# A dynamic convolution in eight 64x32 array tiles instead of four 128x32 ones, from block 8 on

## The chip, the cores and the metric

The kernel runs on one core of one Trainium2 chip. A core has five engines that run side by side and meet through semaphores: TensorE (PE, matrix products; a weight load, PEld, and a matmul are separate instructions), VectorE (DVE), ScalarE (ACT), GpSimd (POOL) and SyncE (SP), of which the last mostly issues DMAs. SBUF is the on-chip memory of 128 partitions. TensorE writes into PSUM[...]. The metric is the device time of one execution in microseconds (us). Before the change it is 747.56 us, the median of three runs (747.36 to 747.77).

## The reference

The input x has 8 sequences of 4096 tokens with 192 channels in 8 heads of 24. Each token has, per head, seven weights of its own; they go through a softmax and weigh the token and the six before it. What results goes through a feed-forward network with a squared ReLU.

```python
w = exp(weight_gen - max);  w = w / (sum(w) + 1e-9)        # (B, S, 8 heads, 7 taps)
out = einsum('bshk,bskhg->bshg', w, windows_of_7(x))       # causal, zeros ahead of the start
h = maximum(out.reshape(-1, 192) @ w_in, 0)                # (32768, 2048)
return h * h @ w_out                                       # (32768, 192)
```

## The kernel before

**Ranges and blocks.** The 32768 tokens are cut into 64 ranges of 512 tokens (`TB`). Blocks 0 and 1 (`BLOCKS`) have one range each, blocks 2 to 32 two. The first range of a two-range block goes to partitions 0 to 63 of the convolution's result y and the second to partitions 64 to 127 (`half`), for three groups of 64 channels (`NK`).

**Convolution as matmuls.** A range is covered by five tiles of 128 tokens (`NT`), which start 104 tokens apart (`STEP`), 24 tokens ahead of the range; each gives 104 output tokens (96 the last). For one tile the convolution is a product of x (tokens on partitions, channels as the stationary columns) with a band matrix bd: column c holds, for one head, the seven weights of output token c at the rows of the tokens that it takes. `st_band` (L338) makes bd on VectorE, by multiplying the weights wr, broadcast, with the constant `mask`, which has ones in a band seven rows wide. Two neighbouring heads lie interleaved in bd's columns, so a matmul reads every second element. Heads of 24 channels don't match strips of 32: for each strip `conv_pieces` (L370) gives first a matmul over 32 channels with the later head's band, and then one over the first 8, 16 or 24 channels with the earlier head's band, which overwrites those rows. Each is a matmul that starts and stops by itself.

**Array tiles before.** A conv matmul (L416) uses all 128 rows of the array and 32 of its columns, at `tile_position=(0, p0)`, where `p0 = RT * half + 32 * (q % 2)` takes four values: four column tiles, used in turn. A two-range block has 5 tiles x 3 channel groups x 2 heads x 4 = 120 matmuls, into two PSUM tiles yp of two banks each. ScalarE then copies them to y in fp16 (L432), the first 128x1024, the second 128x512.

**Feed-forward.** A unit u (`st_unit`, L437) makes 128 of the 2048 hidden channels for the block's 1024 tokens: six matmuls h (L446) of 64 rows and 512 columns, pairs of row halves side by side in different PSUM banks, then the ReLU to t on ScalarE (L455) and the square to g on VectorE (L458). There are 16 units in a two-range block. A step M is half of a quarter of the block's second product: 32 matmuls o (L480) of 64 rows and 192 columns; at the end of a quarter ScalarE (L494) and VectorE (L496) add the two row halves to o_sb, and SP stores them. PSUM has three h tiles of two banks, which h and yp share (`ps_h`), and two banks for o.

**Order.** It is written out by hand: `steady` gives "MuMuuu" three times and then "MuuuMCu" for a block, where C is the convolution of the next block, so it stands between the block's 15th and 16th unit. C is followed by the x loads of the block after (`x_load`, on the POOL queue, with a cast to fp16, into two tiles xt). The bands of the next block (B) stand at units 5 and 9 or 1 and 5, later for a few early blocks. The weights come from a softmax in pieces (E on ScalarE, S on VectorE), which is stored to DRAM (vd) from where SP reads wr in the banded layout (`block_load`, L286): one row of 64 values per token, five tiles in one DMA; where a range starts a sequence, or ends a part of the softmax, the first or last tile has a DMA of its own. For the first blocks the weights go from SBUF to SBUF instead (`wr_load_sbuf`).

**Start-up.** POOL makes `mask` and others with memsets and selects and then clears `v_big`, before the first DMAs that it issues.

Of the kernel before, what the change touches and what calls it, by code (L numbers as in the profile page):

```python
# [9 lines left out]
def kernel(  # L10
# [26 lines left out]
    nc = tc.nc  # L37
    f32 = mybir.dt.float32
    f16 = mybir.dt.float16

    B, S, D = x.shape
    H, KK = weight_gen.shape[2], weight_gen.shape[3]
# [3 lines left out]
    HP = H // 2  # L46

    P = 128
    TB = 512
    NBB = S // TB  # L50
    NSUB = B * NBB
    BLOCKS = [(0, 1), (1, 1)] + [(n, 2) for n in range(2, NSUB, 2)]
# [5 lines left out]
    SL = 8  # L58
    RT = 64
    NK = D // RT  # L60

    NT = 5
    STEP = 104
    BASE = -24
    starts = [BASE + STEP * i for i in range(NT)]
    bounds = [0, 104, 208, 312, 416, TB]

    AluOp = mybir.AluOpType
    AxisX = mybir.AxisListType.X
    ActF = mybir.ActivationFunctionType  # L70

    const = ctx.enter_context(tc.tile_pool(name="const", bufs=1))
# [5 lines left out]
    p_bd = ctx.enter_context(tc.tile_pool(name="p_bd", bufs=3))  # L78
    p_y = ctx.enter_context(tc.tile_pool(name="p_y", bufs=2))
# [4 lines left out]
    ps_h = ctx.enter_context(tc.tile_pool(name="ps_h", bufs=3, space=bass.MemoryType.PSUM))  # L84
# [5 lines left out]
    w_i = const.tile([P, WQ, 2, NQ + NQ // 2], f16, name="w_i")  # L90
    w_o = const.tile([P, NF, Dm], f16, name="w_o")
    mask = const.tile([P, P, 2], f16, name="mask")
    swap = const.tile([P, P], f16, name="swap")
    FIRST = 8
    PARTS = {0: (8, 8, 8, 8), 1: (8, 8, 16), 2: (16, 16)}
# [14 lines left out]
    def band_mask():  # L110

        nc.gpsimd.memset(mask, 1.0)
        for sign, base in ((1, 0), (-1, KK - 1)):
            nc.gpsimd.affine_select(
                out=mask, in_=mask, pattern=[[sign, P], [0, 2]], compare_op=AluOp.is_ge,
                fill=0.0, base=base, channel_multiplier=-sign,
            )


# [148 lines left out]
    x_t, wr_t, bd_t, yp_t, y_t, g_t, h_t, t1_t, o_t, o_sb_t = ({} for _ in range(10))  # L268

    def rows(ap2d, t0, width):  # L270

        return bass.AP(
            tensor=ap2d.tensor, offset=ap2d.offset + t0 * width,
            ap=[[width, P], [STEP * width, NT], [1, width]],
        )

    def ends(b):
        rs = PARTS.get(b, (R,))
        return [P * sum(rs[: i + 1]) for i in range(len(rs))]

    def tile_start(j, i):

        t1 = (j % NBB + 1) * TB
        return TB - P if i == NT - 1 and t1 in ends(j // NBB) else starts[i]

    def block_load(j, dst, src, width, eng):  # L286
        t0 = (j % NBB) * TB
        first, last = int(t0 == 0), NT
        if first:
            eng.dma_start(out=dst[:, 0], in_=src[0:P, :])  # L290
        a = t0 + tile_start(j, NT - 1)
        if a != t0 + starts[-1]:
            last = NT - 1
            eng.dma_start(out=dst[:, last], in_=src[a : a + P, :])
        ap = rows(src, t0 + starts[first], width)
        ap = bass.AP(
            tensor=ap.tensor, offset=ap.offset,
            ap=[ap.ap[0], [STEP * width, last - first], ap.ap[2]],
        )
        eng.dma_start(out=dst[:, first:last], in_=ap)  # L300
# [63 lines left out]
    quads = []  # L364
    for q in range(D // 32):
        ha, hb = (32 * q) // G, (32 * q + 31) // G
# [3 lines left out]
    def conv_pieces(j):  # L370


        s0, n = BLOCKS[j]
        th = n * TB // 2
        halves = []
        for half in (0, 1):
            s, a = (s0 + half, 0) if n == 2 else (s0, th * half)
            halves.append([
                (s, i, half, max(bounds[i], a), min(bounds[i + 1], a + th), a)
                for i in range(NT) if bounds[i] < a + th and bounds[i + 1] > a  # L380
            ])
        if n == 2:
            for k in range(NK):
                for later in (True, False):
                    for pair in zip(*halves):
                        for s, i, half, a, b, base in pair:
                            for q in (2 * k, 2 * k + 1):
                                yield later, s, i, q, half, a, b, base
        else:
            for pair in zip(*halves):  # L390
                for later in (True, False):
                    for k in range(NK):
                        for s, i, half, a, b, base in pair:
                            for q in (2 * k, 2 * k + 1):
                                yield later, s, i, q, half, a, b, base

    def st_conv(j):

        n = BLOCKS[j][1]
        th = n * TB // 2  # L400
        per = 1024 // th
        y = p_y.tile([P, NK, TB], f16, name="y")
        y_t[j] = y
        yps = [
            ps_h.tile([P, 2 * TB], f32, name="yp", tag="h") for _ in range(-(-NK // per))
        ]
        for later, s, i, q, half, a, b, base in conv_pieces(j):
            lo = bounds[i]
            hi = lo + (STEP if tile_start(s, i) == starts[i] else bounds[i + 1] - lo)
            _, ha, hb, pre = quads[q]  # L410
            m, h = (32, hb) if later else (pre, ha)
            bd = bd_t[s][:, H * lo : H * hi].rearrange("p (g c e) -> p g e c", g=HP, e=2)
            p0 = RT * half + 32 * (q % 2)
            k = q // 2
            col = th * (k % per) - base
            nc.tensor.matmul(  # L416
                out=yps[k // per][p0 : p0 + m, col + a : col + b],
                lhsT=x_t[s][:, i, 32 * q : 32 * q + m],
                rhs=bd[:, h // 2, h % 2, a - lo : b - lo],
                start=True,  # L420
                stop=True,
                skip_group_check=True,
                tile_position=(0, p0),
            )
        for n, yp in enumerate(yps):
            k0, k1 = n * per, min((n + 1) * per, NK)

            copies = ((k0, k1, nc.scalar.copy),)
            if j == 0:
                copies = ((0, 2, nc.scalar.copy), (2, NK, nc.vector.tensor_copy))  # L430
            for a, b, copy in copies:
                copy(  # L432
                    out=y[:, a:b, 0:th],
                    in_=yp[:, (a - k0) * th : (b - k0) * th].rearrange("p (k c) -> p k c", c=th),
                )
# [70 lines left out]
        )  # L506

    def st_bands(j):
        first = int(j % NBB == 0)
        last = NT - int(tile_start(j, NT - 1) != starts[-1])  # L510
        for tiles in (range(first), range(first, last), range(last, NT)):
            if tiles:
                st_band(j, tiles)

    with nc.allow_low_precision("fp16 matmul pipeline"), tc.manual_schedule():
# [3 lines left out]
        for b in range(B):  # L519
            t0 = 0  # L520
# [25 lines left out]
        s0, s1, s2 = parts[:3]  # L546
# [76 lines left out]
        for n, s in enumerate(parts[4:], 4):  # L623
            b, f = s.b, s.fb
            k = n - min(m for m, p in enumerate(parts) if p.b == b)
# [8 lines left out]
        for j in range(len(plans), NBLK - 1):  # L634
            a = BLOCKS[j + 1][0]
# [61 lines left out]
        for j in range(NBLK):  # L697
# [3 lines left out]
            for step in plans[j].split():  # L701
                kind, n = step[0], int(step[1:] or 0)
# [24 lines left out]
        j = NBLK - 1  # L727
# [44 lines left out]
```

The softmax here doesn't subtract the row's maximum and nothing guards it: scores larger than these inputs give would overflow.

## Time and profile before

| | |
|---|---|
| median of three runs | 747.56 us |
| span of the profiled execution | 746.6 us |
| TensorE clock granted | full, all through |
| busy: PE, PEld, DVE, ACT, POOL | 738.7, 556.1, 621.7, 624.4, 89.3 us |
| h matmuls (L446) | 3168, 380.3 us busy |
| o matmuls (L480) | 8032, 385.4 us busy |
| conv matmuls (L416) | 3864, 52.0 us busy |
| ReLU (L455) / square (L458) | 512 each, 1026 / 687 ns |
| bands (L348) | 89, 149.3 us busy |
| copies of y on ScalarE (L432) | 64, 47.9 us busy |
| instructions read by DMA for PE (queue q8) | 118 packets, 1.93 MB |

The profile is one execution. Busy time of PE is the time in which at least one matmul is in the array by the modelled ends of matmuls; matmuls overlap, so starts tell more than lengths. The chain that ended last is followed back from the last instruction, at each step to what released it or to the instruction before it on its engine. A group row reads: line, engine, operation, output<-input, shape, count | busy us, mean ns of one | idle time of the engine ahead of it, and who ended most of it. The median of runs also holds what lies around the span, 0.9 us.

### The profile page before, as it was taken

The page shows a single profiled execution, that of the slowest core. Times are in us where ns is not written, and L with a number is a line of the kernel's source. Part 1 is how long each engine was busy: PE and PEld are TensorE (multiplying, and loading weights), DVE is VectorE, ACT ScalarE, POOL GpSimd, SP SyncE. Part 2 cuts the span into 40 slices and gives each one's busy share as a digit, 9 for nine tenths or more (in the row PEclk, how much of TensorE's full clock was granted, in tenths as well). Part 3 has the DMA queues.
Part 4 walks back from the last instruction along what each step waited for, and adds up shares of the span by engine and source line. Part 5 has one row for each costly group of instructions (what it writes and reads, how often), then busy time and mean ns, then how long its engine had stood idle before and what let it go on. Part 6 is the DMA issues. An engine that isn't in the chain of part 4 may idle for free.

```text
span 746.6 us, 33289 instructions
## 1 busy us (share of the span) xinstructions
PE 738.7 (99%) x15106; PEld 556.1 (74%) x15106; DVE 621.7 (83%) x1002; ACT 624.4 (84%) x755; POOL 89.3 (12%) x130
## 2 busy tenths in 40 slices
PE   8999999999999999999999999999999999999998
PEld 4767777777777778777877777777778777777787
DVE  5999998998889888887889888898888987677853
ACT  4998888898888888888888888888888888888884
POOL 7322220101101100011000110001100011000000
PEclk9999999999999999999999999999999999999999
DMA  7745444436554234643245442265341354432312
GB/s 214 121 97 119 80 86 99 99 72 139 94 118 80 73 59 80 139 79 73 40 80 139 94 72 56 48 139 108 59 80 46 59 108 80 60 70 52 53 46 65
DMA packets 122169, 64.81 MB, mean 87 GB/s; under 512 B 83849, under 2 KB 118636, under 8 KB 121516
## 3 DMA queue, kind: packets, MB, share of 16 engines
q1 hardware_dynamic: 77708, 45.66, 22.3%
q0 software_dynamic: 44176, 16.93, 20.5%
q8 instruction: 118, 1.93, 1.1%
q14 instruction: 23, 0.19, 0.1%
q10 hardware_dynamic: 144, 0.10, 0.0%
HBM read 48.61 MB, written 28.70 MB: 104 GB/s over the span
## 4 chain that ended last, share of the span: by engine, by line
PE 91%; DVE 4%; DMA 2%; ACT 2%; issue 1%; DVEq 0%; ACTq 0%; SPq 0%
PE o L480 43%; PE h L446 42%; PE yp L416 6%; DVE bd L348 2%; DVE g L458 1%; ACT t L455 1%; DMA vd<-v_big 1%; DMA wr<-v_first 1%; DMA wg<-in_weight_gen_dram 0%; DVE v_big L239 0%; ACT ex L217 0%; DVE o_sb L496 0%; DVE ssum L224 0%; DVE rcp L231 0%; DVE v_first L239 0%
## 5 line engine op out<-in xcount | busy, mean ns | idle before, releaser
L455 ACT ACTIVATE t<-h 128x1024 f16<-128x1024 f32 x512 | 496.7, 1026 | 64.5 <-PE h L446 63.9
L458 DVE TENSOR_TENSOR g<-t 128x1024 f16<-128x1024 f16 x512 | 334.1, 687 | 99.1 <-ACT t L455 96.4
L480 PEld LDWEIGHTS <-g 64*128 64x128 f16 (+1 forms) x8032 | 352.5, 94 | 54.2 <-issue 3.8
L480 PE MATMUL o<-w_o,g 64*128 64x192 f16 (+1 forms) x8032 | 385.4, 243 | 0.2
L446 PE MATMUL h<-y,w_i 64*128 64x512 f16 (+1 forms) x3168 | 380.3, 370 | 1.9 <-ACT t L455 0.8
L446 PEld LDWEIGHTS <-w_i 64*128 64x128 f16 x3168 | 162.5, 94 | 117.5 <-issue 5.2
L348 DVE TENSOR_TENSOR bd<-wr,mask 128x4160 f16<-128x4160 f16 (+3 forms) x89 | 149.3, 1701 | 4.2 <-DMA wr<-v_first 4.2
L300 POOL DMA_DIRECT2D xt<-in_x_dram x62 | 51.6, 836 | 445.6 <-PE yp L416 422.7
L494 ACT COPY o_sb<-o 128x384 f32<-128x384 f32 x129 | 62.2, 482 | 33.7 <-PE o L480 33.7
L496 DVE TENSOR_TENSOR o_sb<-o,o_sb 128x384 f32<-128x384 f32 x123 | 68.2, 554 | 8.2 <-ACT o_sb L494 5.6
L432 ACT CAST y<-yp 128x1024 f16<-128x1024 f32 (+1 forms) x64 | 47.9, 799 | 15.1 <-PE yp L416 15.0
L416 PE MATMUL yp<-bd,xt 128*32 128x104 f16 (+8 forms) x3864 | 52.0, 208 | 0.7 <-DVE bd L348 0.3
L416 PEld LDWEIGHTS <-xt 128*32 128x32 f16 (+3 forms) x3864 | 46.2, 92 | 7.1 <-issue 6.4
L239 DVE TENSOR_TENSOR v_big<-ex,rcp 128x112 f16<-128x112 f32 (+1 forms) x136 | 27.3, 264 | 2.1 <-DMA vd<-v_big 0.9
L217 ACT ACTIVATE ex<-wg 128x448 f32<-128x448 f32 (+2 forms) x44 | 27.2, 618 | 2.1 <-DMA wg<-in_weight_gen_dram 2.1
L224 DVE TENSOR_REDUCE ssum<-ex 128x64 f32<-128x448 f32 (+2 forms) x44 | 26.1, 593 | 2.6 <-ACT ex L217 2.6
L231 DVE RECIPROCAL rcp<-ssum 128x64 f32<-128x64 f32 (+2 forms) x44 | 23.7, 539 | 1.5
L290 POOL DMA_DIRECT2D xt<-in_x_dram x7 | 3.8, 548 | 137.1 <-PE yp L416 137.1
L330 POOL DMA_DIRECT2D wr<-v_first x31 | 16.8, 559 | 16.1 <-DVE v_first L239 15.9
L544 PE MATMUL wp<-warm 128*128 128x512 f16 x39 | 10.7, 440 | 1.3 <-DVE warm L536 1.3
L544 PEld LDWEIGHTS <-warm 128*128 128x128 f16 x39 | 4.2, 111 | 7.1 <-issue 2.6
L239 DVE TENSOR_TENSOR v_first<-ex,rcp 128x112 f16<-128x112 f32 (+1 forms) x48 | 9.1, 255 | 0.3
(25 smaller groups left out, 28.7 us busy)
## 6 DMA issues: line engine op xcount, KB each, us to landing
out_dram<-o_sb SPq DMA_DIRECT2D x63, 384.0 KB, 3.0
xt<-in_x_dram POOLq DMA_DIRECT2D x42, 240.0 KB, 6.2
wg<-in_weight_gen_dram SPq DMA_DIRECT2D x4, 1064.0 KB, 8.3
xt<-in_x_dram POOLq DMA_DIRECT2D x20, 192.0 KB, 5.4
wr<-vd SPq DMA_DIRECT2D x38, 80.0 KB, 3.9
vd<-v_big SPq DMA_DIRECT2D x5, 512.0 KB, 5.5
wg<-in_weight_gen_dram SPq DMA_DIRECT2D x5, 392.0 KB
wg<-in_weight_gen_dram SPq DMA_DIRECT2D x3, 616.0 KB, 4.5
```

The source lines that it names most:

```text
L217: nc.scalar.activation(out=self.ex[:, lo:hi].rearrange("p r g k e -> p (r g) k e"), in_=self.wg[:, lo:hi].rearrange("p r (g e) k -> p (r g ...
L239: eng.tensor_tensor(out=bass.AP(tensor=v.tensor, offset=v.offset + lo * H * SL + lo % SL * 2 + g * SL * 2, ap=[list(v.ap[0]), [H * SL + 2, ...
L300: eng.dma_start(out=dst[:, first:last], in_=ap)
L348: nc.vector.tensor_tensor(out=bd_t[j][:, H * lo : H * (lo + len(tiles) * n)].rearrange("p (g m c) -> p g m c", g=shape[1], c=2 * SL), in0= ...
L416: nc.tensor.matmul(out=yps[k // per][p0 : p0 + m, col + a : col + b], lhsT=x_t[s][:, i, 32 * q : 32 * q + m], rhs=bd[:, h // 2, h % 2, a - ...
L432: copy(out=y[:, a:b, 0:th], in_=yp[:, (a - k0) * th : (b - k0) * th].rearrange("p (k c) -> p k c", c=th),)
L446: nc.tensor.matmul(out=h[:, half, jj * th : (jj + 1) * th], lhsT=w_in_chunk(u * per + jj, slot, half), rhs=y_t[j][r0 : r0 + RT, k, 0:th], ...
L455: nc.scalar.activation(out=t1, in_=h, func=ActF.Relu)
L458: nc.vector.tensor_tensor(out=g, in0=t1, in1=t1, op=AluOp.mult)
L480: nc.tensor.matmul(out=oo[:, cc * Dm : (cc + 1) * Dm], lhsT=g[r0 : r0 + n, cc * P : (cc + 1) * P], rhs=w_o[r0 : r0 + n, fc, :], start=(fc ...
L494: nc.scalar.copy(out=o_sb, in_=o[0][:, c])
L496: nc.vector.tensor_tensor(out=o_sb, in0=o[1][:, c], in1=o_sb, op=AluOp.add)
```

## The change

From block 8 on (ranges 14 to 63, 25 blocks) the convolution is laid out otherwise; blocks 0 to 7 stay.

- A range is cut into two segments of 256 tokens (`SEG`). Partitions 0 to 63 of xt and wr hold tiles of the first segment, 64 to 127 of the second. A tile has 64 tokens (`RT`) and gives 56 outputs (`SSTEP`; 32 the last), after 8 tokens of lead-in; there are again five.
- `split_load` replaces `block_load` for these: one DMA for each segment, with first or last tiles apart where a sequence starts or a part ends; in the first case a memset on POOL clears the eight rows ahead of the sequence.
- `st_split_band` makes a band of 5 x 56 columns for all 8 heads at once, 2240 values per partition for 4160, with `smask`, the diagonal blocks of `mask`, which POOL copies at start-up.
- `st_split_conv` has 240 matmuls of 64 rows for 120 of 128 rows, at `tile_position=(r0, p0)` with r0 0 or 64: eight tiles, used in turn. The row halves write to different PSUM banks (`yp[..., r, ...]`). The first copy of y is issued ahead of the last third of the matmuls; the copies have the same sizes as before.

```diff
+    SPLIT = 8
+    SEG = TB // 2
+    SSTEP = 56
+    LEAD = 8
+    sbounds = [SSTEP * i for i in range(NT)] + [SEG]
...
+        for r0 in (0, RT):
+            nc.gpsimd.tensor_copy(
+                out=smask[r0 : r0 + RT], in_=mask[r0 : r0 + RT, r0 : r0 + RT]
+            )
...
+    def last_shift(j):
+
+        return (RT - sbounds[-1] + sbounds[-2]) if (j % NBB + 1) * TB in ends(j // NBB) else LEAD
+
+    def split_load(j, dst, src, width, eng):
+
+        for r in (0, 1):
+            t0 = (j % NBB) * TB + SEG * r
+            d = dst[RT * r : RT * (r + 1)]
+            first, last = int(t0 == 0), NT
+            if first:
+                nc.gpsimd.memset(d[0:LEAD, 0], 0.0)
+                eng.dma_start(out=d[LEAD:, 0], in_=src[0 : RT - LEAD, :])
+            if last_shift(j) != LEAD:
+                last = NT - 1
+                eng.dma_start(out=d[:, last], in_=src[t0 + SEG - RT : t0 + SEG, :])
+            eng.dma_start(
+                out=d[:, first:last],
+                in_=bass.AP(
+                    tensor=src.tensor,
+                    offset=src.offset + (t0 + SSTEP * first - LEAD) * width,
+                    ap=[[width, RT], [SSTEP * width, last - first], [1, width]],
+                ),
+            )
+
     def block_load(j, dst, src, width, eng):
+        if is_split(j):
+            return split_load(j, dst, src, width, eng)
...
+    def st_split_band(j):
+
+        bd_t[j] = p_bd.tile([P, H * NT * STEP], f16, name="bd")
+        n = H * SSTEP
+        for i0, i1, shift in (
+            ((0, NT, LEAD),) if last_shift(j) == LEAD
+            else ((0, NT - 1, LEAD), (NT - 1, NT, last_shift(j)))
+        ):
+            cols = SSTEP if i1 - i0 > 1 else sbounds[-1] - sbounds[-2]
+            shape = (P, HP * (i1 - i0), cols // SL, 2 * SL)
+            nc.vector.tensor_tensor(
...
+                op=AluOp.mult,
+            )
+
+    def st_split_conv(j):
+
+        s0 = BLOCKS[j][0]
+        y = p_y.tile([P, NK, TB], f16, name="y")
+        y_t[j] = y
+        for k0, k1 in ((0, 2), (2, NK)):
+            yp = ps_h.tile([P, 2, TB], f32, name="yp", tag="h")
+            for k in range(k0, k1):
+                for later in (True, False):
+                    for i in range(NT):
+                        a, b = sbounds[i], sbounds[i + 1]
+                        for half in (0, 1):
+                            for q in (2 * k, 2 * k + 1):
+                                _, ha, hb, pre = quads[q]
+                                m, h = (32, hb) if later else (pre, ha)
+                                for r in (0, 1):
+                                    r0 = RT * r
+                                    p0 = RT * half + 32 * (q % 2)
+                                    col = SEG * (k - k0)
+                                    bd = bd_t[s0 + half][
+                                        r0 : r0 + RT, H * SSTEP * i : H * SSTEP * (i + 1)
+                                    ].rearrange("p (g c e) -> p g e c", g=HP, e=2)
+                                    nc.tensor.matmul(
+                                        out=yp[p0 : p0 + m, r, col + a : col + b],
+                                        lhsT=x_t[s0 + half][r0 : r0 + RT, i, 32 * q : 32 * q + m],
+                                        rhs=bd[:, h // 2, h % 2, 0 : b - a],
+                                        start=True,
+                                        stop=True,
+                                        skip_group_check=True,
+                                        tile_position=(r0, p0),
+                                    )
+            nc.scalar.copy(
+                out=y[:, k0:k1].rearrange("p k (r c) -> p r k c", r=2),
+                in_=yp[:, :, 0 : SEG * (k1 - k0)].rearrange("p r (k c) -> p r k c", c=SEG),
+            )
+
     def st_conv(j):
 
+        if j >= SPLIT:
+            return st_split_conv(j)
...
     def st_bands(j):
+        if is_split(j):
+            return st_split_band(j)
```

## The prediction

> **What bounds the kernel now.** I read the page first: busy shares, then the chain that ended last.
>
> ```profile
> PE 738.7 (99%) x15106; PEld 556.1 (74%) x15106; DVE 621.7 (83%) x1002; ACT 624.4 (84%) x755; POOL 89.3 (12%) x130
> ...
> q8 instruction: 118, 1.93, 1.1%
> ...
> PE 91%; DVE 4%; DMA 2%; ACT 2%; issue 1%; DVEq 0%; ACTq 0%; SPq 0%
> PE o L480 43%; PE h L446 42%; PE yp L416 6%; DVE bd L348 2%; DVE g L458 1%; ACT t L455 1%; DMA vd<-v_big 1%; DMA wr<-v_first 1%; DMA wg<-in_weight_gen_dram 0%; DVE v_big L239 0%; ACT ex L217 0%; DVE o_sb L496 0%; DVE ssum L224 0%; DVE rcp L231 0%; DVE v_first L239 0%
> ...
> L348 DVE TENSOR_TENSOR bd<-wr,mask 128x4160 f16<-128x4160 f16 (+3 forms) x89 | 149.3, 1701 | 4.2 <-DMA wr<-v_first 4.2
> ...
> L416 PE MATMUL yp<-bd,xt 128*32 128x104 f16 (+8 forms) x3864 | 52.0, 208 | 0.7 <-DVE bd L348 0.3
> L416 PEld LDWEIGHTS <-xt 128*32 128x32 f16 (+3 forms) x3864 | 46.2, 92 | 7.1 <-issue 6.4
> ```
>
> TensorE sets the end: 91% of the chain, with no waits worth the name (0.7 us ahead of all conv matmuls). The other engines' shares of the chain lie early: asked by stretches, the chain from 165 us on is TensorE alone but for 0.1% (o 47.6%, h 45.3%, conv 6.5%), and the first changed conv starts at 167 us. So the time is the sum of TensorE's pieces, and only a shorter or longer conv (L416, 6%) can change it much. Then the list of waits of TensorE, which holds only start-up items of 1.3 us or less:
>
> ```profile
> PE wp L544 <- DVE warm L536: 1.3, 1, 1.3
> ...
> PE yp L416 <- DVE bd L348: 0.3, 1, 0.3
> PE yp L416 <- DVE xt L314: 0.3, 1, 0.3
> ```
>
> Then one conv in the timeline (start, length, engine, line):
>
> ```profile
> 302.96 1.45 PEld L416 LDWEIGHTS <-xt 128*32 128x32 f16 x120 [0.16 <-issue]
> 302.96 1.62 PE L416 MATMUL yp<-bd,xt 128*32 128x104 f16 x120
> 303.18 0.50 ACT L494 COPY o_sb<-o 128x384 f32<-128x384 f32 x1
> ...
> 304.14 1.50 ACT L432 CAST y<-yp 128x1024 f16<-128x1024 f32 x2 [0.46 <-PE yp L416]
> ...
> 304.51 0.82 PE L446 MATMUL h<-y,w_i 64*128 64x512 f16 x6
> ```
>
> 120 matmuls, 1.55 us from the first to the next h. From the starts of the single matmuls in the trace, over the 25 convs concerned (blocks 8 to 32): 0.17 us from the last o matmul to the first conv matmul, 1.39 us from the first conv start to the last, 0.14 us to the next h; 1.70 us in all, 42.4 us in the kernel. The 120 are 30 rounds over four column tiles, so a round takes 46 to 48 ns, which is 104 columns at the 0.42 ns per column that the 512-column h matmuls show (0.215 us start to start for a pair), plus a few ns. **The conv is bound by the columns that pass through a tile**, not by issue: its 240 instructions come at one per 5.8 ns.
>
> [...] The trace agrees that row halves run side by side: the two L446 matmuls of a pair start 3 ns apart and together take 0.215 us. [...] single bursts start an instruction every 1.7 ns (2 to 3.4 ns for a weight load and its matmul), but the densest stretch of 24 starts (block 0's conv) takes 81 ns, 3.4 ns each. [...] the queue line above agrees on the block (118 x 256 is the program), but no run shows how far ahead it reads.
>
> **The change, part by part.**
>
> *Matmuls.* 120 of 128 rows and mostly 104 columns become 240 of 64 rows and 56 columns (32 in the last range), 30 rounds of eight tiles. Columns alone: the 56-column matmuls that blocks 0 and 1 already have follow each other on one tile at 26 ns, 48-column ones at 25 ns (the starts at 13.8 and 15.3 us), so 24 x 26 + 6 x 25 = 0.77 us. Issue: 240 pairs. At the best burst pace, 3.3 ns a pair, 0.80 us;[...] at the densest stretch of 24, 6.8 ns a pair, 1.63 us (too high as far as the array, not the issue, limited that stretch). I take 0.96 us,[...] between the two measured ends.
>
> *Switching.* The array changes mode into and out of the conv as before: 0.17 us in. Out: the last matmul has 32 columns for 96, 27 ns less, 0.11 us.
>
> *Sum.* 0.17 + 0.96 + 0.11 = 1.24 us against 1.70: 0.46 us a conv, 25 convs, **11.4 us**. Ends: 0.80 us gives 15.4 us; 1.63 us costs 25 x (0.24 - 0.03) = 5 us.
>
> *Bands.* From the rows by form, a 4160-column band takes 2.314 us and a 768-column one 0.550: 0.52 ns a column. 2240 columns then take 1.32 us, so about 1.0 us less for each of 50 ranges, 50 us off VectorE. Worth nothing: it isn't on the chain after start-up. It widens the cover of a band, which is due a third of the way through a block and used at its end.
>
> *Copies of y.* Same two ScalarE copies, 1.01 and 0.59 us, the first now issued amid the matmuls, in the same order on ScalarE. It can start once two thirds of the conv is done, then 0.3 us earlier. y is next needed by the new block's first h, after u15 (0.65 us) and an M step (1.32 us); two copies take 1.50 us. Still covered by some 0.5 us; without the cover each conv would lose the shortfall. The h buffers are safe in the same way: the conv takes two of three, as before.
>
> *Loads.* Same bytes and rows, in twice as many DMAs of 64 partitions: on POOL 0.84 us (L300) becomes two of perhaps 0.55 to 0.8 us (the 128-row, one-tile form takes 0.55), up to 1.6 us a conv more on a queue that idles 21 us before each x load; x is used a block later (22.6 us; landing takes 6). On SP two to four more issues of about 0.5 us for wr, with stores and later loads queued behind them; nobody waits for those within a block. The new memsets of eight rows stand on POOL ahead of x loads: the wr one waits for a band a block ago, the xt one for the conv that the x load waits for anyway. Start-up: two small smask copies ahead of v_big's memset, where POOL then idles 1.79 us. All nothing.
>
> The profiled execution spans 746.6 us and the median of the runs is 747.56, 0.9 us around the span. 746.6 - 11.4 + 0.9 = **736.1 us**.
>
> **Rivals.** *Instruction reading becomes the bound (slower).* The conv's 480 instructions (16.4 KB per 256) would pass in 0.96 us. By the queue line, 1.1% of 16 engines x 746.6 us over 118 packets is 1.11 us per 256 instructions, 4.3 ns each. If the store held just a block beyond the current one, the conv would outrun it: it crosses into the held block, uses it up in half a microsecond, and stands until the next has been asked for and read. At 4.3 ns for all 480, 2.06 us: 25 x (2.06 - 1.39 - 0.03) = 16 us more, 763.5 us. It decides the sign from a conv of 1.41 us on. For: this burst is twice as long and fast as any now[...]. Against: packets start with up to 113 instructions of the next block already started, so more than one block is held[...]. *Issue is slower than the bursts* (6 to 7 ns a pair, or weight loads of two row halves don't overlap): 1.4 to 1.7 us, 747 to 754 us. *Pace between*: 5 to 5.8 ns, 740 to 746 us. *The gain is taken back by ScalarE*: it is busy 19.2 of each 22.6 us, so 22.1 us still holds it; the same time would result only if h buffers came late after each conv; 747.5 us. *Full pace*, 0.80 us: 732.2 us.
>
> **How the numbers follow.** Columns and issue as estimated, including full pace (731.5 to 740): 0.46. Pace between, 740 to 746: 0.05. Within 0.2% (746.1 to 749.1; about what a measurement of this kernel can tell from no change): 0.06, from the issue and ScalarE cases. Instruction reading (752 to 775): 0.30. Slow issue above 749: 0.13. So faster 0.51, same 0.06, slower 0.43. The likeliest case's own range is 731.5 to 740; for 8 in 10 I reach up through most of the reading case: 731.5 to 767.
>
> **What would show it.** The first-to-last start of a conv falls from 1.39 to about 0.96 us, at an even pace over its 30 rounds; the L416 row shows some 6864 matmuls (3864 + 25 x 120), the chain's share for conv falls from 6% to about 4 to 5%, and PE's wait list stays empty. VectorE falls by 50 us, to 570, with no effect. Wrong if the starts show holes of a microsecond in some convs and not in others, each filled when an instruction packet has landed (reading); an even pace of 6 ns or more (issue); or new idle of PE on y or t after the convs (ScalarE).

## The result and the profile after

The changed kernel takes 846.41 us (median of four runs, 842.43 to 850.16) against 747.66 us for the kernel before on the same chip: a ratio of 1.132, with a 95% interval of 1.1279 to 1.1361. I had forecast 736.1 us and a range up to 767. The sign was that of the slower rival, instruction reading, and its size was six times what I had given it.

The profile page after: engines, the queue that reads TensorE's instructions, the chain that ended last, and the groups of the conv and of the bands.

```profile
PE 771.9 (92%) x18106; PEld 585.5 (70%) x18106; DVE 580.5 (69%) x996; ACT 627.6 (75%) x755; POOL 120.0 (14%) x202
...
q8 instruction: 141, 2.31, 1.1%
...
PE 85%; issue 8%; DVE 4%; DMA 1%; ACT 1%; DVEq 0%; ACTq 0%; SPq 0%
...
L487 PE MATMUL yp<-bd,xt 64*32 64x56 f16 (+7 forms) x6000 | 57.4, 188 | 47.9 <-issue 47.9
L487 PEld LDWEIGHTS <-xt 64*32 64x32 f16 (+3 forms) x6000 | 51.7, 86 | 54.9 <-issue 54.4
...
L449 DVE TENSOR_TENSOR bd<-wr,smask 128x2240 f16<-128x2240 f16 (+2 forms) x58 | 65.5, 1141 | 0.0
```

TensorE still sets the end, but 8% of the chain is now "issue", time in which it waited for nothing that the profile shows; before it was 1%. The conv's matmuls (L487 and its weight loads) carry most of it: 47.9 us of idle time ahead of them, where all conv matmuls before had 0.7 us. 3000 matmuls more and their 3000 weight loads are 6000 instructions, and the reading queue shows 23 packets of 256 more (141 for 118). The bands fell by 51 us, as forecast (98.4 us in two groups, L449 and L390, for 149.3), VectorE as a whole by 41 (580.5 for 621.7), and nothing came of it.

The list of waits, with us in total, times and the longest, has these items for TensorE. Before, its matmuls had no item on issue at all, and its weight loads 6.4 us for the conv and 3.8 for o:

```profile
PEld L487 <- issue: 54.4, 50, 2.6
...
PE yp L487 <- issue: 47.9, 25, 2.5
...
PEld L586 <- issue: 21.4, 36, 2.7
...
PE o L586 <- issue: 11.7, 8, 2.3
```

25 times is once in each changed conv: a hole of up to 2.5 us. Another 8 stand ahead of o matmuls. One conv in the timeline (start, length, engine, line; the idle time before it and its cause in brackets):

```profile
272.39 0.66 PE L586 MATMUL o<-w_o,g 64*128 64x192 f16 x12
272.98 1.41 PE L487 MATMUL yp<-bd,xt 64*32 64x56 f16 x154
276.71 1.00 PE L487 MATMUL yp<-bd,xt 64*24 64x32 f16 x86 [2.32 <-issue]
277.64 1.41 PE L552 MATMUL h<-y,w_i 64*128 64x512 f16 x6
278.84 0.69 PE L586 MATMUL o<-w_o,g 64*128 64x192 f16 x6
```

154 matmuls run, TensorE stands for 2.3 us with everything in place, then the other 86 run. And the six h matmuls after it span 1.41 us, for 0.82 before. The view by windows says why (stretch, its us, TensorE's busy us and matmuls, clock granted as a share of full, DMA share, GB/s; the first two rows follow this hole, the third the hole of 2.73 us that ends at 224.55):

```profile
276.71:277.74 1.03, 1.03 (x88) 1.00 0.57 92
277.74:281.15 3.41, 3.41 (x36) 0.50 0.66 70
224.55:227.96 3.41, 3.41 (x106) 1.00 0.61 75
```

For 3.41 us the granted clock is half, and h pairs that are 0.215 us apart at full clock are 0.42 us apart there. It doesn't follow every long hole: from the first changed conv to the last matmul there are nine such stretches and 22 holes of over 2 us.

**Where each microsecond went.** In what follows a block of work is one of the kernel's blocks of ranges, and a block of 256 is a block of instructions as they are read. From the starts of single matmuls, from the first changed conv to the last matmul of the kernel:

| us | before | after | difference |
|---|---|---|---|
| 25 convs, without holes of over 0.3 us | 42.4 | 55.4 | +12.9 |
| holes inside the convs (25) | 0 | 52.5 | +52.5 |
| holes of over 0.5 us in the steps behind (9) | 0 | 14.8 | +14.8 |
| h and o | 533.9 | 547.2 | +13.3 |
| sum | 576.4 | 669.9 | +93.5 |

The profiled spans differ by 94.1 us (746.6 and 840.7), so the table holds nearly all. Three things are to be explained: a conv without its holes takes 2.21 us (0.17 in, 1.94 from first to last, 0.11 out) where I had 1.24; the holes; and the slower h and o behind them.

**A closer look at the starts.** Of the conv above, the start of every eighth matmul, in ns from the first:

```
0  38  65  92 | 224  291  357  423  490  557  624 ... 1224 | hole | 3750  3787  3819  3851 | 4012  4078  4145 ...
```

Some 30 matmuls with their weight loads start at 3.3 ns a pair, from the second round of eight on in 26 to 27 ns, which is the pace of one tile (26 ns from one 56-column matmul to the next in the starts of the kernel before). Between the 30th and the 33rd there is a pause of about 0.1 us; in all 25 convs its longest gap, 68 to 101 ns, stands behind the 32nd matmul, which with the weight loads is the 64th instruction. From there to the hole every round of eight takes 66 to 67 ns: 8.3 ns a pair, 4.2 ns an instruction. After the hole it is the same again: some 30 matmuls at that quick pace, a pause, the rest at 8.3 ns, but for one longer round. Of all rounds from the sixth on in the 25 convs, holes left out, 83% take 64 to 69 ns; the rest include the quicker rounds behind holes. I read this as 64 instructions that had gathered while TensorE was busy or standing, and a supply of 4.2 ns each behind them; the trace shows the starts alone, not where instructions wait.

The holes: counting TensorE's instructions (weight loads, matmuls and a few semaphore instructions) from the first in the trace, every hole of over 0.5 us from the first changed conv on stands behind number 256 p + 193, but for the drain at the kernel's end. Some of them, with the landing of the last packet of instructions before the hole's end:

```
behind instruction   rest of 256   hole us   ends at us   last packet landed at us
8897                 193           2.73      224.55       223.12
11201                193           2.49      276.71       275.24
13505                193           0.72      328.87       327.56
13761                193           2.20      332.87       331.60
33729                193           2.48      776.81       775.35
```

So instructions run out at the end of a block of 256, and come back 1.3 to 1.6 us after a packet has landed. Convs stand differently to the blocks (a block of work is 1184 instructions of TensorE, which 256 doesn't divide), which is why the holes in convs differ from 0.37 to 2.74 us.

### The profile page after: what moved, and what is told of

The parts are those of the page before. It is cut to its first block, busy times and chain, and to the rows that moved or that the text cites. A ratio compares the mean times of both kernels' runs of the same rounds, so it can differ in the third digit from the quotient of the medians.

```text
span 840.7 us, 39522 instructions
## 1 busy us (share of the span) xinstructions
PE 771.9 (92%) x18106; PEld 585.5 (70%) x18106; DVE 580.5 (69%) x996; ACT 627.6 (75%) x755; POOL 120.0 (14%) x202
## 4 chain that ended last, share of the span: by engine, by line
PE 85%; issue 8%; DVE 4%; DMA 1%; ACT 1%; DVEq 0%; ACTq 0%; SPq 0%
PE o L586 40%; PE h L552 37%; PE yp L487 7%; DVE bd L390 1%; DVE g L564 1%; PE yp L522 1%; ACT t L561 1%; DMA vd<-v_big 1%; DMA wr<-v_first 0%; DMA wg<-in_weight_gen_dram 0%; DVE v_big L250 0%; ACT ex L228 0%; DVE ssum L235 0%; DVE rcp L242 0%; DVE v_first L250 0%
## 5 line engine op out<-in xcount | busy, mean ns | idle before, releaser
L564 DVE TENSOR_TENSOR g<-t 128x1024 f16<-128x1024 f16 x512 | 343.1, 689 | 230.3 <-ACT t L561 226.6
L586 PEld LDWEIGHTS <-g 64*128 64x128 f16 (+1 forms) x8032 | 360.6, 96 | 71.2 <-issue 21.4
L586 PE MATMUL o<-w_o,g 64*128 64x192 f16 (+1 forms) x8032 | 396.0, 247 | 12.0 <-issue 11.7
L317 POOL DMA_DIRECT2D xt<-in_x_dram x100 | 66.5, 679 | 443.6 <-PE yp L487 397.1
L487 PE MATMUL yp<-bd,xt 64*32 64x56 f16 (+7 forms) x6000 | 57.4, 188 | 47.9 <-issue 47.9
L487 PEld LDWEIGHTS <-xt 64*32 64x32 f16 (+3 forms) x6000 | 51.7, 86 | 54.9 <-issue 54.4
L496 ACT CAST y<-yp 128x1024 f16<-128x1024 f32 (+1 forms) x50 | 39.2, 800 | 67.2 <-PE yp L487 67.1
L449 DVE TENSOR_TENSOR bd<-wr,smask 128x2240 f16<-128x2240 f16 (+2 forms) x58 | 65.5, 1141 | 0.0
L390 DVE TENSOR_TENSOR bd<-wr,mask 128x3328 f16<-128x3328 f16 (+3 forms) x25 | 32.9, 1356 | 3.9 <-DMA wr<-v_first 3.9
L372 POOL DMA_DIRECT2D wr<-v_first x31 | 16.9, 563 | 15.0 <-DVE v_first L250 14.8
L342 POOL DMA_DIRECT2D xt<-in_x_dram x12 | 10.2, 854 | 50.9 <-PE yp L522 50.9
L538 ACT CAST y<-yp 128x512 f16<-128x512 f32 (+2 forms) x14 | 10.4, 788 | 3.9 <-PE yp L522 3.9
```

The source lines that it names most:

```text
L317: eng.dma_start(out=d[:, first:last], in_=bass.AP(tensor=src.tensor, offset=src.offset + (t0 + SSTEP * first - LEAD) * width, ap=[[width, ...
L390: nc.vector.tensor_tensor(out=bd_t[j][:, H * lo : H * (lo + len(tiles) * n)].rearrange("p (g m c) -> p g m c", g=shape[1], c=2 * SL), in0= ...
L449: nc.vector.tensor_tensor(out=bass.AP(tensor=bd_t[j].tensor, offset=bd_t[j].offset + n * i0, ap=[list(bd_t[j].ap[0]), [2 * SSTEP, shape[1] ...
L487: nc.tensor.matmul(out=yp[p0 : p0 + m, r, col + a : col + b], lhsT=x_t[s0 + half][r0 : r0 + RT, i, 32 * q : 32 * q + m], rhs=bd[:, h // 2, ...
L496: nc.scalar.copy(out=y[:, k0:k1].rearrange("p k (r c) -> p r k c", r=2), in_=yp[:, :, 0 : SEG * (k1 - k0)].rearrange("p r (k c) -> p r k c ...
L564: nc.vector.tensor_tensor(out=g, in0=t1, in1=t1, op=AluOp.mult)
```

## The experiments

**Theory F, the instruction supply**, put together from these starts and holes. (a) Beyond the first 64 instructions of a burst TensorE gets one per 4.2 ns. (b) The block of 256 that runs and the next are at hand; the one after that is asked for when the sequencer (in this theory what takes instructions up to 64 ahead of their start) enters the next, and is there some 3.7 us later, an estimate from the times between starts in the trace of the kernel after. A block that passes in less leaves a hole of the difference. (c) Behind some holes of over 2 us the clock is low for a while (0.50 for 3.41 us above). **Rival A: the layout of the array**, small 64-row tiles or two row halves in banks of their own make conv matmuls slow or stall them. **Rival B: the number of instructions alone**, each costs 4.2 ns and the position in the blocks doesn't matter.

**Half of the instructions.** The conv of the kernel after, with the matmuls of each strip's earlier head left out (so half of the convolution isn't computed): 120 matmuls in eight tiles, as many instructions as before.

```diff
-                for later in (True, False):
+                for later in (True,):
```

> The kernel after, with the earlier head's matmuls left out (so the first 8, 16 or 24 channels of each strip hold the wrong head): 120 matmuls per conv instead of 240, still in all eight 64x32 tiles, with the same loads, bands and copies; 240 instructions per conv, as before. Theory F (the count of instructions is what costs: [...] they come at one per 4.2 ns, and a conv that needs more than the current block of 256 and the next one stands until a third has been read): 32 matmuls at 3.3 ns and 88 at 8.3 ns, 0.96 us from first to last start, no holes; 0.46 us less per conv than before, about 736 us. Theory A (the eight-tile layout itself is slow: row halves that share column strips or PSUM partitions hold each other up, and the loads in halves come late): the holes of about 2 us stay, about 790 us.

742.69 us, ratio 0.9932 (0.9916 to 0.9949), nearly 7 us above F's number. No hole in any conv; it takes 0.17 + 0.97 + 0.12 us without the holes behind it, 8.1 ns a pair on average. But ten holes of 0.3 to 1.1 us, 6.6 us in all, stand behind convs, each at the end of a block of 256. F had left them out. So fewer columns are of use in eight tiles, but not at the array's pace: 120 matmuls at 3.3 ns would take 0.40 us.

**Twice the instructions in the old layout.** The kernel before, with each conv matmul from block 8 on cut in two by columns: 128x32 tiles, four of them, same columns in all.

```diff
-            nc.tensor.matmul(
-                out=yps[k // per][p0 : p0 + m, col + a : col + b],
...
+            cuts = (a, (a + b) // 2, b) if j >= 8 and k >= 0 else (a, b)
+            for c0, c1 in zip(cuts, cuts[1:]):
+                nc.tensor.matmul(
+                    out=yps[k // per][p0 : p0 + m, col + c0 : col + c1],
...
```

> The kernel before, with each conv matmul from block 8 on cut into two of half the columns: 240 matmuls per conv, but in the old layout of four 128x32 tiles, old loads and bands. Theory F: 240 matmuls at 8.3 ns, 2.0 us, with holes of 0.4 to 2.7 us at the ends of blocks of 256 instructions, as in the kernel after: 830 to 850 us. Theory A: only the array's pace counts, 60 rounds of 26 ns, 1.56 us for 1.39: about 752 us.

842.33 us, ratio 1.1265 (1.1246 to 1.1285). The groups of the page:

```profile
L418 PE MATMUL yp<-bd,xt 128*32 128x52 f16 (+9 forms) x6864 | 70.0, 190 | 48.8 <-issue 48.2
```

Nearly the same 48 us of issue idle as after; 25 holes of 0.8 to 2.8 us in the convs (52.9 us), eight behind them (14.8 us), and 8.3 ns a pair beyond the first 32. Nothing of eight tiles, row halves, PSUM banks, loads, bands or copies is in this kernel. Rival A falls: 94 us of loss, for 99 in the kernel after, come with the number of TensorE instructions at that place alone.

**The same instructions in three places.** The kernel after, all 240 matmuls, but the three channel groups as pieces of 80 that stand a few steps apart.

```diff
-        for k0, k1 in ((0, 2), (2, NK)):
+        for k0, k1 in ((piece, piece + 1),):
...
+        spread = "MuMuuu" * 2 + "MuMuuDu" + "MuuDuMuD"
```

> The kernel after, its 240 matmuls in eight tiles unchanged in number, but issued in three pieces of 80 (one for each channel group, each with a PSUM tile and a copy of its own) at three places in the block, 2.6 us or more of other work apart. Theory F: each piece passes without a hole, 32 matmuls at 3.3 ns and 48 at 8.3, 0.5 us, plus 0.28 us to switch in and out: 2.3 us of conv in place of 1.70, 755 to 765 us. Theory A: as slow as the kernel after or slower, since the switches are added: 845 us or more.

769.45 us, ratio 1.0284 (1.0269 to 1.0299). One piece in the timeline, whole, and the group row, with no idle time left ahead of it:

```profile
256.14 0.79 PE L488 MATMUL yp<-bd,xt 64*32 64x56 f16 x80
256.87 0.82 PE L551 MATMUL h<-y,w_i 64*128 64x512 f16 x6
```

```profile
L488 PE MATMUL yp<-bd,xt 64*32 64x56 f16 (+7 forms) x6000 | 59.7, 186 | 0.0
```

77 of the 99 us are gone with no instruction taken away. The clock is full in all four runs (1.0), so (c) goes with the holes. The time is 4 us above F's range since a piece takes 0.62 us from first to last for the 0.5 I had given it.

**160 matmuls, and where they stand.** The kernel before, with only the first channel group's conv matmuls cut in two (160 matmuls, 320 instructions).

```diff
-            cuts = (a, (a + b) // 2, b) if j >= 8 and k >= 0 else (a, b)
+            cuts = (a, (a + b) // 2, b) if j >= 8 and k == 0 else (a, b)
```

> The kernel before, with only the matmuls of the first of three channel groups cut in two from block 8 on: 160 matmuls, 320 instructions per conv. Theory F: the first 80 at 8.3 ns (first 32 faster), the others at the array's 11.6: 1.55 us instead of 1.39, and holes only in those convs where the end of a block of 256 falls early in the conv: some 0.3 to 1 us on average, 757 to 775 us. If read-ahead were three blocks or more, no holes: 751 us. Theory A: 749 us.

751.72 us, ratio 1.0046 (1.0031 to 1.0061), and no hole at all: F's number was missed, and the other reading, three blocks of 256 or more held (751 us), would have fitted. The conv takes 1.88 us, 0.18 more than before. But the count of instructions shows another reading. With 320 in the conv a block of work is exactly 1024 instructions, four blocks of 256, and every conv starts 74 instructions into one. 182 of its instructions then share a block of 256 with 74 instructions of long matmuls ahead of them, and 138 share the next with 118 of long matmuls behind them, so that no block of 256 may pass too fast. If that is so, the same kernel must get holes when only the position is shifted.

**Only the position shifted.** 59 or 91 small warm-up matmuls of 8 columns more at start-up, whose result nobody reads, so that each conv starts 192 instructions into a block, or at its start.

```diff
+        for i in range(59):
+            nc.tensor.matmul(
+                out=wp[:, 0:8], lhsT=warm[:, 0:P], rhs=warm[:, 0:8], start=True, stop=True
+            )
```

> The kernel with 160 matmuls per conv (old layout, first channel group cut in two), unchanged but for 59 matmuls of 8 columns at start-up, while TensorE waits for the first bands: 118 instructions that move every later one against the ends of the blocks of 256 in which instructions are read. There a two-range block of work has 1024 instructions, so all its convs stand alike: by the trace of that kernel 74 instructions into a block of 256, with the new start 192 into one. Theory F (a block is asked for when the sequencer enters the one ahead of it, and is at hand 3.7 us later): the sequencer enters a block as the conv starts and needs the next as the conv ends, 1.7 us later: a hole of 2.0 us after each conv, 800 to 815 us. Theory B (what counts is the number of instructions in a stretch of time, wherever the blocks end): no holes, 752 to 754 us.

> The same with 91 such matmuls, 182 instructions: every conv starts at the start of a block of 256. Theory F: the sequencer, 64 ahead, enters that block 1.5 us before the first conv matmul and needs the next 1.2 us after it: holes of about 1.0 us inside each conv, after its 128th matmul; 775 to 785 us. Theory B: no holes, 752 to 755 us.

810.0 us for the first, ratio 1.0832 (1.0793 to 1.087), and 778.89 for the second, ratio 1.0405 (1.0387 to 1.0423). Start-up work that moved the first conv by 2.3 and 1.5 us has cost 58 and 27 us. In the timeline the first has its hole behind the conv's last matmul, the second behind its 128th:

```profile
298.32 1.78 PE L418 MATMUL yp<-bd,xt 128*32 128x52 f16 x160
302.09 0.82 PE L448 MATMUL h<-y,w_i 64*128 64x512 f16 x6 [1.99 <-ACT y L434]
```

```profile
288.45 1.41 PE L418 MATMUL yp<-bd,xt 128*32 128x52 f16 x128
290.75 0.55 PE L418 MATMUL yp<-bd,xt 128*32 128x104 f16 x32 [0.88 <-issue]
```

In both that is the end of a block of 256: the conv's instructions up to there are 64 + 256 and 256. Rival B falls, and (b) stands. The first fence also shows a trap: its hole is put down to ScalarE's copy of y (40.9 us in all in the list of waits), because that wait ended last by the records; the weight loads of the same h matmuls, which need no y, stand as long (55.8 us on issue). ScalarE does the same copies at the same distance from the conv without any hole in the run unshifted.

**What (b) measures.** In theory F the sequencer is up to 64 instructions ahead of what starts, by the 64 that start in a burst, so I count from the start of the instruction 64 before a block's first to the start of the next block's first. Where there is a hole between, this takes a median of 3.65 to 4.0 us in the kernel after (3.96) and in the runs above with holes; where there is none, the shortest is 4.4 us in the kernel after and in the run with 160 unshifted. The limit isn't sharp: with half the instructions, with three pieces and in the kernel before, single blocks of 256 pass in 3.7 to 3.8 us without a hole. The kernel before was already at the edge: it has two holes of reading, 0.33 us at 259.45 and 0.44 at 621.18, both at the end of a block of 256 and 1.4 to 1.5 us behind a landing.

**A version that keeps the columns and halves the instructions.** The two heads of a strip lie in one band tile, so one matmul of 2 x 56 columns can take both bands with all 32 channels: 120 matmuls, 240 instructions, and the whole convolution is computed. PSUM then holds twice the results; ScalarE copies the later head's half with a scale per partition, and VectorE adds the earlier head's half times another.

```diff
+                            nc.tensor.matmul(
+                                out=yp[p0 : p0 + 32, r, :, a:b],
+                                lhsT=x_t[s0 + half][r0 : r0 + RT, i, 32 * q : 32 * q + 32],
+                                rhs=bass.AP(
+                                    tensor=bd.tensor,
+                                    offset=bd.offset + h // 2 * 2 * SSTEP + h % 2,
+                                    ap=[list(bd.ap[0]), [2 * SSTEP - 1 if h % 2 else 1, 2], [2, b - a]],
+                                ),
...
+            nc.scalar.activation(
+                out=yk, in_=yp[:, :, 1], func=ActF.Copy, scale=side_m[:, 1, k : k + 1]
+            )
+            nc.vector.scalar_tensor_tensor(
+                out=yk, in0=yp[:, :, 0], scalar=side_m[:, 0, k : k + 1], in1=yk,
+                op0=AluOp.mult, op1=AluOp.add,
```

> The kernel after, with the two matmuls per strip of channels merged: one matmul per strip, tile and segment takes both heads' bands (2 x 56 columns, into two ranges of PSUM columns), so that a conv has 120 matmuls in eight tiles, 240 instructions, as the kernel before has. ScalarE takes the later head's columns into y, zero on the rows of the earlier head by a scale per partition; VectorE adds the earlier head's columns, zero elsewhere. Three PSUM tiles instead of two, and the conv stands one M step earlier against the last unit. Theory F: 15 rounds of eight tiles need 0.73 us of array and the 240 instructions 0.97 us, as in the run with the later head alone; 0.44 us less per conv than before, and holes where a block of 256 holds most of a conv, as in that run (6 us in all): 741 to 745 us, faster than both kernels. If the extra 2.1 us per conv of VectorE (as much as the shorter bands gave back) or the third PSUM tile hold up the units after the conv: 748 us or more.

782.25 us, ratio 1.0456 (1.0442 to 1.047). The waits name it:

```profile
PE yp L493 <- ACT t L575: 17.9, 50, 0.4
PE o L600 <- DVE o_sb L616: 10.5, 25, 0.4
```

The conv now takes all three h tiles of PSUM, and behind three units in a row the second and third are still being read by the ReLU: two waits in each conv. Holes of reading are all but gone from this slower order: three of over 0.3 us, 1.3 us in all. I then moved the conv to where ReLUs have been done.

```diff
-        merged = "MuMuuu" * 3 + "MuuuCMu"
+        merged = "MuMuuu" * 3 + "MCMuuuu"
```

> Both heads' bands in one matmul of 2x56 columns, as in the merged kernel before it (120 matmuls and 240 instructions of a conv), with the conv now between two steps of h, so that the ReLUs that read the conv's PSUM tiles have been done before it starts, and the evacuation of y has four steps of o behind it. Theory of the instruction supply (two blocks of 256, 4.2 ns an instruction beyond the first 64): the conv takes 0.17 + 0.97 + 0.12 = 1.26 us as in the run with one head's matmuls left out, or up to 0.31 + 0.97 + 0.13 = 1.41 with another h pair ahead of it, and leaves 6 to 10 us of holes in the steps behind it: 740 to 748 us. Theory that the wider evacuation is a limit by itself, wherever it stands: o or the next conv waits for VectorE, 755 to 785 us.

772.33 us, ratio 1.032 (1.0299 to 1.0342). The conv is down to 0.17 + 1.02 + 0.13 us, and a wait has opened elsewhere:

```profile
PE o L600 <- DVE g L578: 22.3, 20, 1.2
```

The rival's number, 755 to 785 us, came true, but not for its reason, the wider copy of y. A piece of the softmax, about 2 us of VectorE, stands ahead of a block's last unit; the next block's second step M needs that unit's square g, and the conv during which VectorE used to do the piece is gone from there. So the softmax pieces had to move too: to the sixth unit (two pieces to the sixth and tenth), and the bands to the second and third; or, in another version, the conv to the third quarter and the pieces to the thirteenth unit.

```diff
+            double = [j for j, u in times if (j, 9) in times and (j, 15) in times]
+            times = [
+                (j, u if j + 1 < SPLIT or u == 0 else {9: 5, 15: 9}[u] if j in double else 5) for j, u in times
+            ]
...
+            if j + 1 >= SPLIT and not small:
+                us = (1, 2)
```

> The run before it (conv between two steps M, both heads in one matmul) lost 22 us where o waits for the square g of a block's last unit: a piece of the softmax stands on VectorE ahead of that unit, and the conv that used to give it time is gone from there. Here the pieces of the softmax stand at the block's sixth unit (two of them at the sixth and tenth), and the bands at the second and third. Theory of the instruction supply: the waits for g go; the conv's gain of about 8 us (1.38 us for 1.70, 25 times) stays, and so do the holes of reading in the steps behind it (some 9 us in the run before): 745 to 751 us. Theory that the wider evacuation of y is the limit wherever it stands: new waits on VectorE or ScalarE in the steps behind the conv, above 758 us.

> The same with the conv in the third quarter of a block, between the steps M ahead of its ninth unit, and the softmax pieces at the thirteenth unit, so that the block ends as it does in the kernel before without its conv. Theory of the instruction supply: as the run beside it, 745 to 751 us, the holes in other places. If the pieces of the softmax at the thirteenth unit still come too close to the block's end: waits of o for g, 755 to 770 us.

The first takes 746.39 us, ratio 0.9979 (0.997 to 0.9987, 13 runs against 15): 0.2% below the kernel before, small but clear of the scatter, and 100 us below the kernel after. The second takes 770.55, ratio 1.0294 (1.0275 to 1.0313); there it isn't g, as I had said it might be, but o that waits for VectorE's o_sb, 14.8 us, and nine holes of reading stay. TensorE's list of the first has nothing of other engines left after start-up, so the wider copy of y, which is still there, isn't a limit by itself:

```profile
PE o L600 <- issue: 4.1, 7, 1.2
PE h L566 <- issue: 1.7, 2, 0.9
...
PE yp L493 <- issue: 0.9, 2, 0.6
```

Its convs take 33.1 us without holes, 9.4 less than before, and eleven holes at ends of blocks of 256, in and behind convs, take 9.5 us back. So the cheaper conv and its holes cancel here; where the small gain left comes from isn't shown.

## Why the prediction was wrong

**What bounds the kernel: right.** TensorE alone set the end before and after; 41 us less of VectorE, two smask copies, twice the loads and an earlier copy of y show nowhere in the table. The bands of 2240 columns took 1.315 us each, as I had worked out.

**The columns: right, and beside the point.** From the second to the fourth round a round of eight takes 26 to 27 ns in the conv shown, the pace of the 56-column matmuls that I had read at start-up; the row halves run side by side. It holds for some 30 matmuls of 240 at the start of a conv, and again behind its hole.

**Switching: right.** 0.17 us in and 0.11 out, as priced.

**The step that failed is the supply of instructions, in two terms.** The profiled run of the kernel after (842.43 us) lies 106 us above the forecast of 736.1. The first term is "Issue": "I take 0.96 us", an estimate between two measured ends that no trace had shown. It took 1.94 us from first to last, holes left out: 24 us more than priced over 25 convs. The second is the time in which TensorE stands for instructions, which the sum put at nothing because "more than one block is held". It was 67 us of holes, and 13 us of half clock that they brought with them. Together that is nearly all of the 106.

*Issue.* Both measured ends were wrong as ends. The burst of 3.3 ns a pair and the densest stretch of 24 starts, 3.4 ns an instruction, came, by theory F, out of the 64 instructions that had gathered beforehand; no conv of the kernel before was bound by supply (its rounds of four took 46 to 48 ns, 11.6 ns or more a pair), so none showed the supply's pace of 4.2 ns an instruction, 8.3 ns a pair. In the kernel after no conv holds the 3.3 ns a pair of its head beyond the 32nd matmul. The rival "Issue is slower than the bursts" had the right sign, but stopped at 7 ns a pair. I had also given an even pace over 30 rounds as the sign; the starts have a kink by the 33rd matmul.

*Holes.* "Instruction reading" was named with its mechanism, its sign in the starts ("each filled when an instruction packet has landed") and a chance of 0.30, at 763.5 us; it was expected in some convs and stood in all 25. Two things were wrong. Its price was a rate, 4.3 ns an instruction by the share of the queue, 2.06 us a conv. What counts in theory F is the time from asking to running, about 3.7 us a block by the estimate above, most of it not in the queue line: the packet itself mostly takes 0.9 to 1.2 us, with about a microsecond or more ahead of it and 1.3 to 1.6 us behind. And "more than one block is held", my argument against, was miscounted: I had counted blocks and packets from the first instruction alike, but the boundaries lie 193 beyond a multiple of 256, and the packet whose landing ends a hole is the one that started only 1 us after the block ahead of the hole began (at 274.06 us, with that block's first instruction at 273.07, in the conv shown). So these starts fit one block held beyond the running one and no more. At 4.2 ns, 256 instructions pass in 1.1 us, far less than the 3.7. The two holes of reading in the kernel before (0.33 and 0.44 us) could have been seen in its starts, though not in its list of waits.

**What no case had.** Holes behind the convs (14.8 us), since a block's shortfall may fall due after the conv that caused it; and the clock. The nine stretches at half clock account for the slower h and o: the nine blocks of work that hold one take 13.7 us more for h and o than in the kernel before, the other sixteen 0.4 us less. All nine start a whole number of times 3.41 us apart, so that a grid of 3.41 us can be laid over the trace. In the nine grid stretches just ahead of them the gaps of over 0.3 us between matmul starts come to 2.15 to 2.68 us, in all others from the first changed conv to the last matmul to 2.11 us at most. The runs with twice the instructions (2.15 against 1.93) and shifted by 118 (2.18 against 2.13) part in the same way. The boundary shifts by up to 0.1 us with how the gaps are summed. What counts in these runs, then, is how much of the standing falls into one stretch: the hole of 2.73 us ahead of 224.55 lies across a boundary, 1.30 and 1.43 us, and left the clock full, while 2.15 us within one stretch of 3.41 were enough elsewhere. The four runs of the kernel after differ with it: 842.43, 844.07, 848.75 and 850.16 us have mean clocks of 0.982, 0.980, 0.976 and 0.970.

**Still open.** Why TensorE takes 1.3 to 1.6 us to go on after a packet has landed, why a microsecond passes before a packet starts, and what sets the 4.2 ns. No run here varied any of them.

## What to carry to other kernels

Count TensorE's instructions as well as its columns. In these runs a matmul with its own weight load cost 8.3 ns beyond the first 32 pairs of a burst, with 52 columns in four tiles and with 56 in eight. So compare 8.3 ns with what a matmul's columns cost when they are spread over the tiles in use: 104 columns in four tiles took 11.6 ns and were the limit, 56 columns in eight tiles took 3.3 ns and were not. Then see how fast each run of 256 instructions passes: under some 4 us TensorE mostly stood here until the next block of 256 was there (single ones of 3.7 to 3.8 us passed). It helped to spread the burst among long matmuls (769.45 us for 846.41) and to make fewer and wider matmuls (746.39), and where the blocks of 256 end was alone worth up to 58 us. An edit far away that adds or removes TensorE instructions moves all later ends, as the 118 and 182 at start-up did, so compare instruction counts before you explain a time by anything else.

## What the runs showed of the hardware

- In the convs of the kernel after TensorE's instructions came at about 4.2 ns each (66 to 67 ns for eight pairs) after the first 64, in eight tiles of 64 rows; in four tiles of 128 rows, with twice the instructions, it was 8.3 ns a pair too.
- In the kernel after all 33 holes of over 0.5 us between matmul starts, from the first changed conv on, stood at ends of blocks of 256 instructions; from 64 instructions ahead of a block to the start of the next it took a median of 3.96 us where there was a hole. TensorE went on 1.3 to 1.6 us after the packet had landed.
- The same kernel body took 751.7, 778.9 and 810.0 us, depending on where its convs lay in the blocks of 256; the start-up work that moved them took 2.3 us at most.
- In the kernel after the granted clock was half for 3.41 us after each stretch of a 3.41 us grid in which TensorE's gaps came to 2.15 us or more (nine), and full after all others from the first changed conv to the last matmul (2.11 us at most). Each of the nine cost h and o 1.2 to 1.7 us.
